# Dealing routing's small VectorE operations out between large ones, with PSUM as a single tile, in a long convolution with routed experts

## Chip, cores and metric

The kernel runs on one core of a Trainium2 chip. The metric is the device time of one execution in microseconds, the median of several.

## What is computed

A long convolution over four batches of 11456 rows by 128 columns, gated by its own input, feeds a mixture of eight experts of which each row takes one. Cut to what matters:

```python
def _attn_ref(x, v, pos_emb, w1, w2):
    h_filt = (np.maximum(pos_emb @ w1, 0.0) @ w2) * np.exp(-0.01 * pos)[:, None]
    u = x * v
    Uf = np.fft.rfft(u, n=2 * S, axis=1)
    Hf = np.fft.rfft(h_filt, n=2 * S, axis=0)
    y = np.fft.irfft(Uf * Hf[None], n=2 * S, axis=1)[:, :S, :]
    return x * y
...
def _moe_ref(x, modality_id, w_gate, modality_bias, w1, w2):
    logits = x @ w_gate + modality_bias[modality_id]
    e_idx = np.argmax(logits, axis=1)
    probs = softmax(logits)
    gate_w = probs[np.arange(N), e_idx]
    for e in range(8):
        mask = e_idx == e
        out[mask] = gate_w[mask, None] * (np.maximum(x[mask] @ w1[e], 0) @ w2[e])
```

## The kernel before

The Fourier transforms are done as matrix products in two levels, an outer one and a middle one. The program is a row of stages: an outer stage, then a middle stage (which works on the spectrum), then the next outer stage, and so on over the four batches, and the experts at the end. An outer stage b does two things at once: the inverse outer transform of batch b - 1, with its gating and its routing, and the forward outer transform of batch b. Three of them (b = 1, 2, 3) are full; the first has only a forward half, the last (b = 4) only an inverse half.

A full outer stage has 16 steps, t = 0 to 15, and a tail of four. In the code, q is such a step's block and o a group, two blocks that are routed together. Each step has on TensorE:
- `turn`: 16 transposes of the middle stage's result into PSUM (wt, L694), which ScalarE copies out (L695);
- `half`: eight transposes of gated rows (xT, L751), copied out by ScalarE (L753);
- `forward`: 64 small matmuls (s, L495), copied out as A (L498);
- `inverse`: py, eight records (L703).

VectorE makes the product of two loaded tiles ready for `forward` (`product`: mul, add, sub, L480, L483, L484), and from py the inverse result: add, sub and the gate with x (L707, L708, L709); the gate writes one of the three buffers xo. Before the add ScalarE copies half of py to y (L706).

Every two steps one group is routed. TensorE computes the logits pl (L759) and turns them (lt, L766), VectorE adds the bias (lg, L772). Then `choice` (L775) runs on VectorE in one piece: mx (L780), dl (L782, written over lg), sco (L787), mb (L789), oh (L790), sc (L792), se (L796), sum (L797) and inv (the reciprocal, L802), with exp (L784) and the row numbers tok (L800) on ScalarE. oh marks the chosen expert of each row, sc its running count. `send` (L813) sums both over the rows on TensorE (pr, L818 to L823); VectorE makes places out of it: ro (L825), base (L826), ro2 (L827) and ix (L829). SP stores the gated rows (`store`, L809, which gives xo back) and the places (`places`, L837), and loads the tiles of coming steps (L475, L688).

The order of the work is set by a table, OUTER, that gives each of these functions a number of steps after its block and a place in the step; a Timeline sorts by them, and each engine runs its instructions in that order. `paced` (L459) ties the scattering of rows of an earlier batch, on GpSimd, to certain VectorE operations.

```python
OUTER = ("turn0:0 turn1:0 lturn:3 biased:3 half:2 product:0 forward:1 choice:3 "
         "inverse:0 logits:2 send:4 load_x:-1 load:-2 store:4 places:5")
...
banks.append(cv.enter_context(tc.tile_pool(name="ps", bufs=4, space=PSUM)))
pairs = cv.enter_context(tc.tile_pool(name="pp", bufs=2, space=PSUM))
```

PSUM is given out by these two pools: four single banks, in turn, to every user of `bank` (wt, xT, pl, lt, pr), and two pairs of banks to the users of `pair` (s, py).

## Time and profile before

| | us |
|---|---|
| median of three runs | 2072.83 |
| lowest and highest | 2069.47, 2073.29 |
| the profiled execution, its own time | 2074.09 |
| its span in the trace | 2072.3 |
| TensorE busy | 1958.3 (94%) |
| VectorE busy | 1752.4 (85%) |
| ScalarE busy | 1284.4 (62%) |
| GpSimd busy | 1169.4 (56%) |
| mean granted TensorE clock | 0.982 |

The profile is of one execution. Its span leaves out the little that lies before the first and after the last recorded instruction. An engine's share is an average over stages that differ; the timelines and the stretches below show single stages.

### The profile page before, as it was taken

The numbers are of one execution on the slowest core, as the hardware profiler recorded it, in microseconds if no ns is written. First come the engines' busy times: TensorE is split into PE (matmuls) and PEld (weight loads), VectorE is DVE, ScalarE is ACT, GpSimd is POOL, SyncE is SP. The second block draws the span as 40 slices with busy tenths as digits, with TensorE's granted clock in tenths as the row PEclk, the third lists the DMA queues.
The fourth block names the chain that finished last, engine by engine and source line by source line (L and its number), as shares of the span: only waits on it lengthen the run. The fifth ranks groups of instructions, "written<-read, shape, count | busy, mean of one in ns | idle before, by whom it ended". The sixth has DMA issues, their size and how long they took to land. (4 is left out here: it accounts for less than half of the span.)

```text
span 2072.3 us, 50243 instructions
## 1 busy us (share of the span) xinstructions
PE 1958.3 (94%) x17646; PEld 1554.1 (75%) x17646; DVE 1752.4 (85%) x2612; ACT 1284.4 (62%) x2404; POOL 1169.4 (56%) x1054
## 2 busy tenths in 40 slices
PE   8899898999989998999789999999999999999997
PEld 8688665776667665776468888877888888888897
DVE  6599899999999899996678888897888778878886
ACT  5555675457744675456456666666666666666675
POOL 0144004766678476974456678786555555555654
PEclk9999999999999999999899999999999999999998
DMA  8565688889988898856787456654645555555421
GB/s 319 184 191 173 231 280 268 268 264 314 327 270 253 280 339 288 283 183 179 199 248 205 97 127 138 133 124 103 118 97 97 97 100 98 96 98 100 86 40 29
DMA packets 610842, 379.46 MB, mean 183 GB/s; under 512 B 424026, under 2 KB 542005, under 8 KB 610585
## 3 DMA queue, kind: packets, MB, share of 16 engines
q1 hardware_dynamic: 587193, 328.61, 58.2%
q0 software_dynamic: 23104, 47.34, 6.6%
q8 instruction: 141, 2.31, 0.5%
q14 instruction: 116, 0.95, 0.2%
q10 hardware_dynamic: 288, 0.25, 0.1%
HBM read 272.74 MB, written 103.70 MB: 182 GB/s over the span
## 5 line engine op out<-in xcount | busy, mean ns | idle before, releaser
L1094 ACT ACTIVATE hh<-ph 128x512 fp32r<-128x512 f32 x724 | 434.0, 599 | 323.2 <-PE ph L1091 320.2
L1095 DVE SCALAR_TENSOR_TENSOR hl<-ph,hh 128x512 fp32r<-128x512 f32 x724 | 488.5, 680 | 164.4 <-ACT hh L1094 155.6
L276 POOL DMA_INDIRECT xs<-back,to x360 | 405.4, 1126 | 319.9 <-DVE se L797 107.9
L1160 POOL DMA_INDIRECT out<-ot,x x362 | 373.3, 1031 | 160.2 <-issue 36.7
L1089 PE MATMUL ph<-xh,wh 128*128 128x512 f32 (+1 forms) x792 | 298.0, 376 | 8.3 <-ACT wh L1060 8.3
L1091 PE MATMUL ph<-xl,wh 128*128 128x512 f32 (+1 forms) x792 | 296.2, 374 | 9.0 <-POOL xl L1077 9.0
L1115 PE MATMUL po<-hl,wh 128*128 128x512 f32 (+1 forms) x792 | 295.6, 373 | 0.9 <-DVE hl L1095 0.6
L1090 PE MATMUL ph<-xh,wl 128*128 128x512 f32 (+1 forms) x792 | 295.6, 373 | 0.0
L1113 PE MATMUL po<-hh,wh 128*128 128x512 f32 (+1 forms) x792 | 295.1, 373 | 0.2 <-ACT hh L1094 0.2
L1114 PE MATMUL po<-hh,wl 128*128 128x512 f32 (+1 forms) x792 | 294.7, 372 | 0.0
L673 ACT COPY A<-pw 128x512 f32<-128x512 f32 (+1 forms) x184 | 97.1, 580 | 188.1 <-PE pw L669 188.1
L1077 POOL TENSOR_TENSOR xl<-xT,xh 128x512 fp32r<-128x512 f32 (+1 forms) x77 | 96.2, 1250 | 203.2 <-ACT xh L1073 203.2
L669 PEld LDWEIGHTS pw<-work 64*128 64x128 f32 x2856 | 167.2, 189 | 32.1 <-ACT work L607 19.2
L625 PE MATMUL pz<-A,work 128*64 128x256 f32 x1440 | 181.1, 394 | 8.3 <-DMA work<-in_c_to 5.0
L638 POOL TENSOR_TENSOR work<-work 128x512 f32<-128x512 f32 (+1 forms) x92 | 115.3, 1253 | 129.0 <-DVE work L634 128.4
L669 PE MATMUL pw<-work 64*128 64x128 f32 x2856 | 181.6, 279 | 4.7 <-POOL work L655 4.3
L1091 PEld LDWEIGHTS ph<-xl,wh 128*128 128x128 f32 x792 | 150.5, 190 | 37.0 <-POOL xl L1077 10.8
L1089 PEld LDWEIGHTS ph<-xh,wh 128*128 128x128 f32 x792 | 150.5, 190 | 33.6 <-ACT wh L1060 8.5
L1115 PEld LDWEIGHTS po<-hl,wh 128*128 128x128 f32 x792 | 150.0, 189 | 29.8 <-DVE hl L1095 4.2
L1090 PEld LDWEIGHTS ph<-xh,wl 128*128 128x128 f32 x792 | 150.6, 190 | 26.1 <-DVE wl L1061 0.4
L1113 PEld LDWEIGHTS po<-hh,wh 128*128 128x128 f32 x792 | 150.0, 189 | 26.1 <-ACT hh L1094 0.7
L1114 PEld LDWEIGHTS po<-hh,wl 128*128 128x128 f32 x792 | 150.0, 189 | 25.7
(181 smaller groups left out, 3613.9 us busy)
## 6 DMA issues: line engine op xcount, KB each, us to landing
work<-hs SPq DMA_DIRECT2D x66, 512.0 KB
work<-in_x SPq DMA_DIRECT2D x64, 512.0 KB
work<-in_xd SPq DMA_DIRECT2D x58, 512.0 KB
work<-in_v SPq DMA_DIRECT2D x51, 512.0 KB
xr<-xo SPq DMA_DIRECT2D x64, 365.6 KB
back<-xr SPq DMA_DIRECT2D x120, 195.0 KB
work<-in_c_to SPq DMA_DIRECT2D x88, 256.0 KB
blocks<-xs SPq DMA_DIRECT2D x328, 64.0 KB
```

The source lines that it names most:

```text
L276: s = pool.indirect_dma_start(out=xs, out_offset=bass.IndirectOffsetOnAxis(ap=ix, axis=0), in_=src, in_offset=None, bounds_check=E * R - 1 ...
L625: pe.matmul(z[64 * s:64 * s + 64, t, r], k["b"][:, t, s, r], A[:, :, 4 * g + 2 * t + s], start=True, stop=True)
L669: pe.matmul(v[s][:, t, blk], k[of][at, t, r, blk], k["c"][at, t, r], start=i == 0, stop=i == len(terms) - 1)
L1089: pe.matmul(p, k[0, "h"][:, f:f + D], k["xh"], start=True, stop=False)
L1090: pe.matmul(p, k[0, "l"][:, f:f + D], k["xh"], start=False, stop=False)
L1091: pe.matmul(p, k[0, "h"][:, f:f + D], k["xl"], start=False, stop=True)
L1094: act.activation(hh, ph, AF.Relu)
L1095: steps.append(ins_of(dve.scalar_tensor_tensor(hl, ph, 0.0, hh.bitcast(F32), op0=ALU.max, op1=ALU.subtract)))
L1113: pe.matmul(po, k[1, "h"][:, f], hh[:, t], start=g == 0, stop=False)
L1114: pe.matmul(po, k[1, "l"][:, f], hh[:, t], start=False, stop=False)
L1115: pe.matmul(po, k[1, "h"][:, f], hl[:, t], start=False, stop=g == NCH - 1)
L1160: s = pool.indirect_dma_start(out=out, out_offset=bass.IndirectOffsetOnAxis(ap=ix, axis=0), in_=src, in_offset=None, bounds_check=N - 1, o ...
```

## The change

The full outer stages no longer use the table for their compute. A function step(t) writes each step's instructions in an order written out by hand; loads, stores and places stay in the table. The first and last outer stages keep the table.

*VectorE.* `product`, the inverse, `choice` and `send` are given as lists of single operations, which step(t) interleaves: between two of the large operations (three of the product, three of the inverse) stands one, at times two, of the small ones. One group's routing now takes two steps. In the even step: mx and dl, with the sums (ro, base, ro2, ix) of the group before; in the odd step: sco, se, mb, sum, oh, inv, sc. Before, all of `choice` stood in the even step, and the sums after the odd step's gate. In the two pieces below, of VectorE in the middle of a full stage, L480 to L484 (after: L505 to L507) are the product, L787 to L802 (after: L840 to L860) the routing, and L746 is the inverse's add. Before:

```order
L480 TENSOR_TENSOR work<-work 128x1024 [waits DMAHW2_49,DMAHW1_49]
L483 TENSOR_TENSOR work<-work 128x512 [waits DVE_49]
L484 TENSOR_TENSOR work<-work 128x512
L780 TENSOR_REDUCE mx<-lg 109x16
L782 TENSOR_TENSOR lg<-lg,mx 109x128 [waits DVE_49]
L787 SCALAR_TENSOR_TENSOR sco<-lg,small 109x128 [waits DVE_49]
L789 TENSOR_REDUCE mb<-sco 109x16 [waits DVE_49]
L790 SCALAR_TENSOR_TENSOR oh_102<-sco,mb 109x128 [waits DVE_49]
L792 SCALAR_TENSOR_TENSOR sc_104<-small,oh_102 109x128 [waits DVE_49]
L796 TENSOR_REDUCE se<-ex 109x16 [waits Activation_49]
L797 TENSOR_SCALAR se<-se 109x16 [waits DVE_49]
L802 RECIPROCAL xo_91<-se 109x4x4 [waits DVE_49]
```

After, from ix of the even step to the odd step's add:

```order
L896 TENSOR_REDUCE ix_94<-ro 109x4x4
L505 TENSOR_TENSOR work<-work 128x1024 [waits DMAHW7_49,DMAHW6_49]
L840 SCALAR_TENSOR_TENSOR sco<-lg,small 109x128 [waits DVE_49]
L855 TENSOR_REDUCE se<-ex 109x16 [waits Activation_49]
L506 TENSOR_TENSOR work<-work 128x512 [waits DVE_49]
L849 TENSOR_REDUCE mb<-sco 109x16 [waits DVE_49]
L856 TENSOR_SCALAR se<-se 109x16 [waits DVE_49]
L507 TENSOR_TENSOR work<-work 128x512
L850 SCALAR_TENSOR_TENSOR oh_102<-sco,mb 109x128 [waits DVE_49]
L860 RECIPROCAL xo_91<-se 109x4x4 [waits DVE_49]
L852 SCALAR_TENSOR_TENSOR sc_104<-small,oh_102 109x128 [waits DVE_49]
L746 TENSOR_TENSOR work<-psum,work 128x512 [waits Activation_49]
```

The seven operations from sco to sc have moved from the even step into the odd step, between the three of the product; inv comes ahead of sc; ix now stands after the even gate.

*TensorE.* pr stays in the odd step, behind py and pl; sc is now computed in the same step. On TensorE at the odd step's end (py is L703, after L735; pl L759, after L808; pr L818 to L823, after L883 to L888; wt L694, after L719) before:

```order
L703 MATMUL py<-work,inv 64x512 x3
L759 MATMUL pl<-work,wg 32x436 x4
L818 LDWEIGHTS both
L818 MATMUL pr<-oh_102,both 128x128
L820 LDWEIGHTS both
L820 MATMUL pr<-sc_104,both 128x128
L823 LDWEIGHTS both
L823 MATMUL pr<-sc_104,both 128x8
L694 MATMUL wt<-ident,A 90x128 x8
L694 MATMUL wt<-ident,A 90x128 [waits Activation_49]
```

After:

```order
L735 MATMUL psum<-work,inv 64x512 x3
L808 MATMUL psum<-work,wg 32x436 [waits Activation_49] x2
L808 MATMUL psum<-work,wg 32x436 x2
L883 LDWEIGHTS both
L883 MATMUL psum<-oh_102,both 128x128 [waits DVE_49]
L885 LDWEIGHTS both
L885 MATMUL psum<-sc_104,both 128x128 [waits DVE_49]
L888 LDWEIGHTS both
L888 MATMUL psum<-sc_104,both 128x8
L719 MATMUL psum<-ident,A 90x128 [waits Activation_49]
```

The order is the same, but pr's matmuls with oh and with sc have become waits for VectorE, and wt waits for ScalarE once for each half.

*PSUM.* One tile holds all eight banks, and each user has banks of its own: pairs in banks 0 to 3, singles in 4 to 7, in the full outer stages wt and s in pairs of 4 to 7, py always in banks 0 and 1, xT in 2 and 3, pl and lt in 2, pr in the last columns of 3.

*Forms.* wt is copied by two copies of 1024 columns a step (before: four of 512). The xT transposes of 109 rows become two, of 64 and of 45 rows, so 16 in a step, in two banks, with one copy for each bank.

The buffers of mx, mb and se go from two to one; ro shares a buffer with sco, before with ex. The diff, cut:

```diff
-        banks.append(cv.enter_context(tc.tile_pool(name="ps", bufs=4, space=PSUM)))
-        pairs = cv.enter_context(tc.tile_pool(name="pp", bufs=2, space=PSUM))
+        psum = cv.enter_context(tc.tile_pool(name="ps", bufs=1, space=PSUM)).tile(
+            [D, 8, 512], F32, name="psum")
...
+        def single(name):
+            return psum[:, 4 + next_of("single", 4)]
+
         def pair(name):
-            return pairs.tile([D, 2, 512], F32, tag="pp", name=name)
+            at = 2 * next_of("pair", 2)
+            return psum[:, at:at + 2]
+
+        def upper(name):
+            at = 4 + 2 * next_of("upper", 2)
+            return psum[:, at:at + 2]
...
-                    p = pair("s1")
+                    p = (upper if b else pair)("s1")
...
             def turn(q, blk):
+                last = b == nb - 1
+                p = None if last else upper("wt")[0:N1]
                 for c in range(2):
-                    p = bank("wt")
+                    pc = bank("wt")[0:N1] if last else p[:, c]
                     for j in range(4):
-                        pe.transpose(p[0:N1, D * j:D * j + D], A[:, blk, :, 8 * q + 2 * j + c], ident)
-                    act.copy(w_t[q % 2][blk][:, c], p[0:N1])
+                        pe.transpose(pc[:, D * j:D * j + D], A[:, blk, :, 8 * q + 2 * j + c], ident)
+                    if last:
+                        act.copy(w_t[q % 2][blk][:, c], pc)
+                if not last:
+                    act.copy(w_t[q % 2][blk], p)
...
-                py = pair("py")
+                py = psum[:, 0:2]
...
             def turn(o, half):
...
+                rows = (slice(0, 64), slice(64, PU))
+                pt = [psum[:, 2 + k, 0:8 * (at.stop - at.start)].rearrange("p (w h n) -> p w h n", w=2, h=4)
+                      for k, at in enumerate(rows)]
                 for way in range(2):
-                    pt = bank("xT")
                     for h in range(4):
-                        pe.transpose(pt[:, PU * h:PU * h + PU], xo[0:PU, way, half, h, 0:D],
-                                     ident[0:PU, 0:PU])
-                    act.copy(xT_t[:, 2 * way + half].rearrange("p h n -> p (h n)"),
-                             pt[:, 0:4 * PU])
+                        for p, at in zip(pt, rows):
+                            pe.transpose(p[:, way, h], xo[at, way, half, h, 0:D], ident[at, at])
+                xT = xT_t.rearrange("p (w s) h n -> p w s h n", w=2)[:, :, half]
+                for p, at in zip(pt, rows):
+                    act.copy(xT[:, :, :, at], p)
...
-            line.stages(at, NQ, LAST if b == nb else OUTER, todo,
-                        lambda name: 2 if name in LATE else 0, when)
+            if b == nb:
+                line.stages(at, NQ, LAST, todo, lambda name: 2 if name in LATE else 0, when)
+                return
+            line.stages(at, NQ, OUTER, {n: todo[n] for n in LATE}, lambda name: 2, when)
+            line.put(at - 2, lambda: product(0))
+            line.put(at - 1, lambda: product(1))
+            chosen, sums = {}, {}
+
+            def step(t):
+                o, odd = t // 2 - 2, t % 2
+                here = 0 <= o < NO
+                if t < NQ:
+                    turn(t, 0)
+                    turn(t, 1)
+                if 0 <= t - 2 < NQ:
+                    rturn((t - 2) // 2, t % 2)
+                if here and odd:
+                    chosen["exp"]()
+                    chosen["tok"]()
+                if 0 <= t - 1 < NQ:
+                    transform(t - 1)
+                if here and not odd:
+                    lturn(o)
+                p = psteps(t) if 2 <= t < NQ else [lambda: None] * 3
+                c = lambda *names: [chosen[n]() for n in names] if here and odd else None
+                r = lambda k: sums.pop(k)() if k in sums and not odd else None
+                p[0](), c("sco", "se"), r(0)
+                p[1](), c("mb", "sum"), r(1)
+                p[2](), c("oh", "inv", "sc"), r(2)
+                if here and not odd:
+                    biased(o)
+                    chosen.update(csteps(o))
+                i = isteps(t) if t < NQ else [lambda: None] * 3
+                e = lambda name: chosen[name]() if here and not odd else None
+                i[0](), e("mx")
+                i[1](), e("dl")
+                i[2](), r(3)
+                if odd and 0 <= (t - 3) // 2 < NO and t >= 3:
+                    logits((t - 3) // 2)
+                if here and odd:
+                    sums.update(enumerate(ssteps(o)))
+                    if t > NQ:
+                        for k in range(4):
+                            sums.pop(k)()
+
+            for t in range(TAIL + 1):
+                line.put(at + t, lambda t=t: step(t))
```

## Rows read from the trace of the kernel before

**Rows 1.** The page's first part: busy time, share of the span, instructions by engine
```profile
PE 1958.3 (94%) x17646; PEld 1554.1 (75%) x17646; DVE 1752.4 (85%) x2612; ACT 1284.4 (62%) x2404; POOL 1169.4 (56%) x1054
```

**Rows 2.** The stretches view: length, busy (count) by engine, TensorE clock, DMA share, GB/s
```profile
sum 313.79, PE 300.25 PEld 205.41 DVE 283.30 ACT 231.51 POOL 138.19; mean PE 100.08 PEld 68.47 DVE 94.43 ACT 77.17 POOL 46.06
...
298.77:313.07 14.30, 13.84 (x219) 9.56 (x210) 13.79 (x26) 10.85 (x22) 0.00 (x0) 1.00 0.78 271
500.51:558.85 58.34, 55.66 (x840) 38.34 (x832) 55.09 (x104) 43.66 (x86) 40.89 (x32) 1.00 0.96 327
732.56:790.73 58.17, 55.44 (x840) 38.33 (x832) 55.12 (x104) 43.65 (x85) 42.21 (x32) 1.00 0.98 338
229.59:270.13 40.54, 39.13 (x603) 27.45 (x603) 34.28 (x58) 30.73 (x60) 0.00 (x0) 1.00 0.73 249
```

**Rows 3.** VectorE's timeline in one pair: start, duration, line, tiles, count [idle before]
```profile
302.45 0.69 DVE L707 TENSOR_TENSOR work<-py,work 128x512 f32<-128x512 f32 x1
...
305.76 0.38 DVE L829 TENSOR_REDUCE ix<-ro 109x16 int32<-109x128 f32 x1
...
306.25 1.22 DVE L480 TENSOR_TENSOR work<-work 128x1024 f32<-128x1024 f32 x1
...
308.11 0.69 DVE L484 TENSOR_TENSOR work<-work 128x512 f32<-128x512 f32 x1
308.71 0.36 DVE L780 TENSOR_REDUCE mx<-lg 109x16 f32<-109x128 f32 x1
309.11 0.29 DVE L782 TENSOR_TENSOR lg<-lg,mx 109x128 f32<-109x128 f32 x1
...
311.68 0.63 DVE L707 TENSOR_TENSOR work<-py,work 128x512 f32<-128x512 f32 x1
...
313.07 1.23 DVE L709 TENSOR_TENSOR xo<-work 128x1024 f32<-128x1024 f32 x1
```

**Rows 4.** TensorE's timeline of the same pair (a row may hold several instructions)
```profile
299.85 1.94 PE L703 MATMUL py<-work,inv 90*64 90x512 f32 x8 [0.20 <-ACT A L498]
...
302.65 0.22 PE L820 MATMUL pr<-sc,both 109*128 109x128 bf16 x1
...
302.74 2.11 PE L694 MATMUL wt<-ident,A 128*90 128x128 f32 x16
304.68 0.66 PE L766 MATMUL lt<-ident,work 128*109 128x128 f32 x4
305.18 1.03 PE L751 MATMUL xT<-ident,xo 109*128 109x109 f32 x8
306.14 1.47 PE L495 MATMUL s<-fwd,work 64*64 64x90 f32 x64
307.87 1.94 PE L703 MATMUL py<-work,inv 90*64 90x512 f32 x8 [0.26 <-ACT A L498]
```

**Rows 5.** Timelines of VectorE and TensorE in the first stage's tail
```profile
347.60 0.42 DVE L792 TENSOR_TENSOR_SCAN sc<-small,oh 109x128 bf16<-109x128 f32 x1
...
347.63 0.29 PE L818 MATMUL pr<-oh,both 109*128 109x128 bf16 x1 [4.99 <-DVE oh L790]
348.08 0.27 PE L820 MATMUL pr<-sc,both 109*128 109x128 bf16 x1 [0.17 <-DVE sc L792]
```

**Rows 6.** SP's and VectorE's timelines in stages two and three: stores and gates
```profile
534.23 1.80 SPq L809 DMA_DIRECT2D xr<-xo  x2
...
544.65 1.23 DVE L709 TENSOR_TENSOR xo<-work 128x1024 f32<-128x1024 f32 x1 [0.67 <-DMA xr<-xo]
...
766.76 1.83 SPq L809 DMA_DIRECT2D xr<-xo  x2
...
776.02 1.23 DVE L709 TENSOR_TENSOR xo<-work 128x1024 f32<-128x1024 f32 x1
```

**Rows 7.** TensorE's timeline in a middle stage
```profile
400.58 2.95 PE L669 MATMUL pw<-work 64*128 64x128 f32 x48
```

**Rows 8.** ScalarE's timeline in the pair of rows 3
```profile
303.50 2.06 ACT L695 COPY work<-wt 90x512 f32<-90x512 f32 x4 [0.17 <-PE wt L694]
```

More of the change, by code (lines that the diff above doesn't have):

```diff
@@ L200, in bank @@
     def bank(name):
+        if callable(banks[-1]):
+            return banks[-1](name)
         return banks[-1].tile([D, 512], F32, tag="ps", name=name)
@@ L499, in transform @@
                              p[:, :, 0:4 * N1].rearrange("p b (n k) -> p b k n", n=4))
-            return load, product, transform
+            return load, product, transform, product_steps
         def filter_stages():
@@ L763, in logits_turn @@
             def logits_turn(o):
-                pt = kept[o] = bank("lt")
+                pt = kept[o] = psum[:, 2]
                 for h in range(4):
@@ L775, in choice, with choice_steps @@
             def choice(o):
+                steps = choice_steps(o)
+                for name in ("mx", "dl", "exp", "sco", "mb", "oh", "sc", "se", "tok", "sum", "inv"):
+                    steps[name]()
+            def choice_steps(o):
                 i = b * NO + o
@@ L792, in choice, with first_of_best @@
-                dve.tensor_tensor_scan(
-                    sc[0:PU].rearrange("p e c -> p (e c)"), sm("keep")[0:PU],
-                    oh[0:PU].rearrange("p e c -> p (e c)"), 0.0, op0=ALU.mult, op1=ALU.add)
-                se = rt.tile([PU, NC], F32, tag="se", name="se")
-                dve.tensor_reduce(se, ec(ex), axis=AX.X, op=ALU.add)
-                dve.tensor_scalar_add(se, se, 1e-9)
+                own = {}
+                def first_of_best():
+                    own["sco"] = rt.tile([PU, E, NC], F32, tag="sco", name="sco", bufs=1)
+                    dve.scalar_tensor_tensor(own["sco"], lg, 0.0, fst, op0=ALU.is_ge, op1=ALU.mult)
@@ L798, in choice @@
                 xov = xo[0:PU].rearrange("p w s h r -> p h (w s) r")
                 by_h = lambda t: t.rearrange("p (h g) -> p h g", h=4)
-                act.activation(xov[:, :, :, D + 1].bitcast(I32), by_h(sm("tok")[0:PU]), AF.Copy,
-                               bias=float(b * S + 8 * o))
-                paced(dve.reciprocal(xov[:, :, :, D], by_h(se)))
+                return {
+                    "mx": lambda: dve.tensor_reduce(mx, ec(lg), axis=AX.X, op=ALU.max),
+                    "dl": lambda: dve.tensor_sub(lg, lg, wide(mx)),
+                    "exp": lambda: act.activation(ex, lg, AF.Exp),
+                    "sco": first_of_best,
+                    "mb": lambda: dve.tensor_reduce(mb, ec(own["sco"]), axis=AX.X, op=ALU.max),
+                    "oh": lambda: dve.scalar_tensor_tensor(
+                        oh[0:PU], own["sco"], 0.5, wide(mb), op0=ALU.max, op1=ALU.is_equal),
+                    "sc": lambda: dve.tensor_tensor_scan(
+                        sc[0:PU].rearrange("p e c -> p (e c)"), sm("keep")[0:PU],
+                        oh[0:PU].rearrange("p e c -> p (e c)"), 0.0, op0=ALU.mult, op1=ALU.add),
+                    "se": lambda: dve.tensor_reduce(se, ec(ex), axis=AX.X, op=ALU.add),
+                    "sum": lambda: dve.tensor_scalar_add(se, se, 1e-9),
+                    "tok": lambda: act.activation(
+                        xov[:, :, :, D + 1].bitcast(I32), by_h(sm("tok")[0:PU]), AF.Copy,
+                        bias=float(b * S + 8 * o)),
+                    "inv": lambda: paced(dve.reciprocal(xov[:, :, :, D], by_h(se)))}
@@ L813, in send, with send_steps @@
             def send(o):
+                for f in send_steps(o):
+                    f()
+            def send_steps(o):
                 i = b * NO + o
                 oh, sc = oh_t[i % 2], sc_t[i % 2]
-                pr = bank("pr")
+                if banks[-1] is single:
+                    pr = psum[:, 3, 512 - E * NC - E:512]
+                else:
+                    pr = bank("pr")
                 prv = pr[:, 0:E * NC].rearrange("p (e c) -> p e c", e=E)
@@ L839, in places @@
                         ix[64 * blk:64 * blk + HALF].rearrange("p (w m) -> p w m", w=2))
-            return turn, logits, logits_turn, biased, choice, send, store, places
+            return turn, logits, logits_turn, biased, choice, send, store, places, choice_steps, send_steps
         def every_other(f):
@@ L862, in outer @@
             if b < nb:
-                load, product, transform = forward_stages(b)
+                load, product, transform, psteps = forward_stages(b)
                 todo |= {"load": load, "product": product, "forward": transform}
@@ L894, in hyena_moe_kernel @@
         todo = filter_stages()
-        load, todo["product"], todo["forward"] = forward_stages(0)
+        load, todo["product"], todo["forward"], _ = forward_stages(0)
         for name in ("xd", "v"):
```

84 lines of the change are left out of this document (50 added, 34 removed).

## The prediction

> **What bounds the kernel now.** The page's first part comes first: TensorE is busy 94% of the span, VectorE 85% [rows 1]. These are averages over stages with different limits, so next I cut out the stages that the change touches, the three full outer stages, with the view of busy time by stretch: from first to last gate they take 313.79 us together [rows 2], so nothing outside them and their tails can move. After about six steps each settles to a fixed period of two steps (a pair, which routes one group): 14.30 us in the first stage, 58.34 / 4 = 14.59 and 58.17 / 4 = 14.54 in the other two [rows 2]. In the 14.30 us TensorE is busy 13.84 and VectorE 13.79: both nearly full, each waiting now and then for the other. DMA share is 0.78 in the first stage, 0.96 to 0.98 in the others, and TensorE's clock is granted in full in these windows, so the clock is no part of this.
>
> VectorE's timeline shows how a pair is filled [rows 3]. Where an operation does not need its predecessor, it starts about 0.09 us before that one ends (308.11 + 0.69 = 308.80, but mx starts at 308.71). Where it reads the predecessor's result, it starts 0.03 to 0.04 us after the end (308.71 + 0.36 = 309.07, dl at 309.11). So a dependent neighbour costs about 0.12 us more than an independent one.
>
> **VectorE's part of the change.** The two orders show 15 dependent neighbours in a pair before (two in each product and inverse, the rest inside the routing), and 2 after (add to sub to gate of the odd step's inverse). 13 x 0.115 = 1.5 us a pair: VectorE's chain falls from some 14.2 to 12.7 us. If VectorE alone were the bound, 24 pairs would give 36 us. It is not alone.
>
> **TensorE's part.** The xT transposes go from 8 with 109 moving columns, 306.14 - 305.18 = 0.96 us [rows 4], to 16 with 64 and 45, which I call X for one step. No row shows this form, so it is bounded. The nearest row has the same stationary shape (64 x 128) in two row groups, with 128 moving columns: 48 in 2.95 us, some 60 ns each [rows 7]. If moving columns set that time, eight pairs of halves cost 8 x 60 = 0.48 us; if loading the weights does, 16 x 60 = 0.96. The s row bears on it: 64 matmuls with 64 stationary columns take 307.87 - 306.14 - 0.26 = 1.47 us [rows 4], 23 ns each, so twice the columns need at most 46 ns or 0.74 us. I take 0.6, half-way between 0.48 and 0.74, and keep 0.48 and 0.96 as ends. The Trainium skill, "TensorE: Matmul & The Clock Gate", section LDWEIGHTS, says that a weight load costs its columns over 1.2 in nanoseconds and that fewer rows save nothing; with 16 loads of 128 columns in two row groups that would be, as an estimate, 16 x 107 / 2 = 0.85 us. The 60 ns of [rows 7] agree with that page as well as with moving columns, so the row decides nothing between them. TensorE's own work in a pair becomes 13.84 - 2 x 0.93 + 2 x 0.6 = 13.2 us, which is also less than 14.3.
>
> **The new wait.** What decides is where sc now ends. Before, the second half of the routing ran in the even step, and its prefix sums on TensorE (pr) came in the odd step, when sc was long done. Now sco to sc are dealt over the odd step, and pr stands behind py and pl of the same odd step, ahead of the next step's wt. TensorE takes its instructions in order: in the stage's tail it stood 4.99 us in front of pr for oh, and started its second matmul 0.06 us after sc ended (347.60 + 0.42 = 348.02, then 348.08) [rows 5]. Behind pr wait wt, xT, s, lt and py, and behind py waits VectorE's next inverse. That closes a loop of one pair:
> - From the even step's first inverse operation to the end of sc, VectorE runs 16 operations: one inverse, mx, dl, ix, one product, sco, se, mb, sum, oh, inv, sc. The old order has the same ones without ix in a row, 15 of them from 306.25 to the gate that starts at 313.07 and gives way 1.14 later: 7.96 us, 10 of the hand-overs dependent [rows 3]. Without those, 7.96 - 10 x 0.115 = 6.81; ix adds 0.38 - 0.09 = 0.29; and sc counts to its end, 0.09 more: 7.2.
> - Hop to pr 0.06, pr's rest 302.74 - 302.65 = 0.09, wt 1.9 (304.68 - 302.74 = 1.94 here, 1.85 in the other step), X, s 1.47, lt 305.18 - 304.68 = 0.50 [rows 4].
> - py's start to the inverse on VectorE: 302.45 - 299.85 = 2.60 [rows 3, 4].
>
> The sum is 13.82 + X: **14.42 us with X = 0.6**, 14.30 to 14.78 between the ends. So VectorE's saving does not shorten the pair; it turns into a VectorE wait for y of 14.4 - 12.7 = 1.7 us a pair, and TensorE waits for sc.
>
> **PSUM and the merged copies.** The second half of s now writes the banks that the second wt copy empties. Four copies of 512 columns take 2.06 us [rows 8]; as two, I keep 2.06, starting when half of wt (0.93) is done, so done some 3.1 us after wt begins, while s' second half begins at 1.9 + X + 0.74: an X below 0.5 gains nothing. py on one pair of banks waits for the add and sub of the step before, which end some 1.3 us after sc, while wt, xT, s and lt hold py back for 4.6: nothing, and in the odd step the cover is still over a microsecond. ro waits for the xT copies on its bank, by the same 1 ns a column 0.15 + 3.1 + 0.9 = 4.1 us after sc, where VectorE arrives after the odd inverse and p0, 2.6 + 1.1 = 3.7: a few tenths, which come out of its wait for y. exp and tok lie on ScalarE, 10.85 of 14.30 busy [rows 2], before se needs them.
>
> **The store.** inv now comes 5.15 us after the even gate's start (the 7.2 without add and sub, 313.07 - 311.68 - 2 x 0.115 = 1.16, mx 0.27, dl 0.20 and sc 0.42 [rows 3, 5]). The store of a group follows inv on SP's queue, and with three buffers the next even gate needs that one back. Before, inv came a step earlier. In the second stage a store issued at 534.23 gave its buffer back at 544.65, 10.42 later, and VectorE waited 0.67 for it; in the third stage the gate at 776.02 came 9.26 after the issue without a wait [rows 6]. So the second loop is 5.15 + 9.3 to 10.4 = 14.4 to 15.6 in stages 2 and 3. I take 14.7 there, nearer the lower end because only a single gate of [rows 6]'s stage waited at all; the emptier first stage is left to the first loop. places now also waits for ix behind the even gate; behind it on SP stand the loads of the odd step, which have a ring of four units of slack: nothing, or part of the high end.
>
> **The sum.** First six steps: 40.54 us, of which TensorE idles 1.4 [rows 2]; those waits and the smaller xT, which enters from the third step on, give 1.4 to 2.7 back; I take 1.6. But the odd gate of a pair now has seven small operations, sco to inv, in front of it: from dl's end at 309.40 to the add at 311.68 they took 2.28, less six dependent hand-overs 1.6 [rows 3], and that gate comes as much later: zero together. Steady pairs, four a stage: 4 x 0.12 = 0.5 in the first, 4 x (14.7 - 14.56) = 0.5 in each other. Tails: the last group's routing stands a little later before the next stage's products; I choose 0.3 each, between 0 and 0.7. 0.5 + 0.5 + 0.5 + 0.9 = +2.4 us on the profiled execution's 2074.09, which lies 1.26 above the median of 2072.83: **2075 us**, no change that can be told; 0.2% is 4.1 us.
>
> **Rivals.**
> - *The dealing pays in full*: pr does not hold TensorE, and the pair falls to its own 13.2 us. 4 x 1.1 + 8 x 1.35 = 15, with the early steps up to 20: 2053 to 2058. Against it stand the order of pr ahead of wt and [rows 5]. Chance 0.08.
> - *The loop comes out short*: wt 1.85, X 0.5, VectorE's run 7.1, the hop to y 2.55 give 14.1, stages 2 and 3 lose their waits for TensorE's irregular turns (14.56 to 14.2), and the early 1.6 are kept in part. 4 x 0.2 + 8 x 0.4 + 3 = 7: 2064 to 2068. Chance 0.16.
> - *The store loop binds* in stages 2 and 3: slower. Its price is 10.42 + 5.15 - 14.56 = 1.0 a pair, 8 us over eight pairs, plus tails: 2080 to 2084. It decides from a store latency of 9.3 us. For it: DMA share 0.96 and up, and a gate that waited already; against: most stores of before were back without a wait. Chance 0.22.
> - *Weights set xT's time*, X = 0.85 to 0.96: the pair is 14.67 to 14.78, 0.4 to 0.5 over stage 1 and 0.1 to 0.2 over the others, 4 x 0.4 + 8 x 0.2 + 0.9 = 4: 2077 to 2079. The page cited above would have it so. Chance 0.2, over half of it past 0.2%.
> - The forecast itself: 0.34.
>
> **Numbers.** Faster: 0.08 + 0.16 = 0.24. Slower: 0.22 + 0.12 = 0.34. The rest, 0.42, is within 0.2%. The range leaves out the full gain and the worst store latency: 2064 to 2085.
>
> **What would show it.** Right: pairs of 14.3 to 14.7 between gates; a wait of pr's second matmul for sc in each pair; VectorE waiting 1 to 2 us a pair for y, its small operations without idle around them; in stages 2 and 3 gates that wait for the store. The second rival shows as the same waits with shorter pairs. Wrong: pairs near 13.2 without a wait at pr; xT far from 0.5 to 0.9 us a step; a merged copy over 1.1 us; or time moved outside the three stages.

## The result: slower by 1.1%

The changed kernel takes 2093.79 us, the median of four runs (2088.04 to 2100.29), the kernel before 2071.15 (2067.58 to 2073.29) beside it: a ratio of 1.0112, 95% interval 1.0075 to 1.0149, or 22.6 us more. The profiled execution of the change took 2090.47 us, with a span of 2088.7 us and a mean granted TensorE clock of 0.976 (before: 0.982).

The stretches view says where the time went. First the change: the three full outer stages, from first to last gate, each followed by the stretch to the next outer stage's first gate, which holds the stage's tail and the middle stage. (Columns as in [rows 2].)

```profile
230.27:332.28 102.01, 97.03 (x1618) 65.52 (x1614) 87.93 (x167) 74.85 (x121) 5.13 (x4) 1.00 0.78 265
332.28:459.31 127.03, 114.29 (x1489) 87.68 (x1484) 117.36 (x117) 59.19 (x109) 92.77 (x82) 0.97 0.84 270
459.31:569.51 110.20, 101.80 (x1632) 69.25 (x1626) 88.56 (x167) 75.91 (x121) 58.91 (x54) 0.95 0.89 301
569.51:700.35 130.84, 117.26 (x1490) 89.20 (x1486) 117.39 (x118) 59.26 (x109) 91.47 (x79) 0.93 0.80 258
700.35:812.08 111.73, 100.24 (x1630) 68.10 (x1626) 88.43 (x167) 75.47 (x121) 58.25 (x54) 0.97 0.88 295
812.08:945.41 133.33, 117.58 (x1442) 89.22 (x1434) 122.60 (x119) 58.61 (x112) 104.51 (x86) 0.95 0.76 243
```

The same three stretches between the stages, before:

```profile
332.55:459.96 127.41, 116.42 (x1483) 89.60 (x1481) 118.44 (x118) 60.24 (x113) 89.91 (x79) 0.97 0.83 265
565.17:690.42 125.25, 114.73 (x1455) 87.98 (x1446) 118.83 (x119) 59.56 (x112) 91.13 (x78) 0.97 0.84 270
796.04:924.74 128.70, 118.01 (x1453) 88.99 (x1451) 124.76 (x119) 59.00 (x112) 106.80 (x85) 0.97 0.79 249
```

| | before | after | difference |
|---|---|---|---|
| stage 1, first to last gate | 102.96 | 102.01 | -0.95 |
| to the next first gate | 127.41 | 127.03 | -0.38 |
| stage 2 | 105.21 | 110.20 | +4.99 |
| to the next first gate | 125.25 | 130.84 | +5.59 |
| stage 3 | 105.62 | 111.73 | +6.11 |
| to the next first gate | 128.70 | 133.33 | +4.63 |

The six differences add up to 20.0 us. Two things are to be seen. Stage 1's steady pairs came out as they were worked out, and those of stages 2 and 3, with the same instructions, did not. And half of the loss lies after the last gate, where the change moved only a group's routing and the PSUM banks; there TensorE's granted clock is 0.93 and 0.95, before 0.97. (The rest of the program, from the last gate of all, took 1053.48 us instead of 1057.46; the kernel before took 1055.4 there in another profiled execution, so much of this is spread.)

**Stage 1: the loop through pr.** TensorE and then VectorE in one pair of the change:

```profile
301.69 0.22 PE L883 MATMUL psum<-oh,both 109*128 109x128 bf16 x1 [0.61 <-DVE oh L850]
302.14 0.22 PE L885 MATMUL psum<-sc,both 109*128 109x128 bf16 x1 [0.24 <-DVE sc L852]
...
302.23 1.98 PE L719 MATMUL psum<-ident,A 128*90 128x128 f32 x16
304.14 0.71 PE L800 MATMUL psum<-ident,xo 64*128 64x64 f32 x16
304.77 1.47 PE L518 MATMUL psum<-fwd,work 64*64 64x90 f32 x64
...
306.79 1.94 PE L735 MATMUL psum<-work,inv 90*64 90x512 f32 x8
```

```profile
295.05 0.69 DVE L746 TENSOR_TENSOR work<-psum,work 128x512 f32<-128x512 f32 x1 [1.10 <-ACT work L738]
...
301.71 0.38 DVE L852 TENSOR_TENSOR_SCAN sc<-small,oh 109x128 bf16<-109x128 f32 x1
...
306.32 0.29 DVE L892 TENSOR_TENSOR ro<-psum,base 109x128 f32<-109x128 f32 x1 [0.53 <-ACT work L803]
...
309.43 0.69 DVE L746 TENSOR_TENSOR work<-psum,work 128x512 f32<-128x512 f32 x1 [1.14 <-ACT work L738]
```

The pairs, from even gate to even gate, are 14.40 us, three times running, and then 14.45. TensorE waits 0.61 us for oh and 0.24 for sc, then runs wt (302.23 to 304.14, 1.91), xT (304.14 to 304.77, X = 0.63), s, lt and py; VectorE waits 0.53 us for the xT copy ahead of ro and 1.14 for y. From the add at 295.05 to sc's end at 302.09 are 7.04 us (7.2 in the prediction), from py at 306.79 to the next add at 309.43 2.64 (2.60). The small operations now stand without idle between the large ones: VectorE is busy 87.93 us in the stage where it was 94.50 us, and the stage is only 0.95 us shorter.

**Stages 2 and 3: the gate waits for the store.** Pairs there are 15.63, 17.00, 16.76, 15.99 and 18.09, 15.97, 16.97, 15.98 us. VectorE's gates and SP's queue in stage 2:

```profile
513.02 1.23 DVE L742 TENSOR_TENSOR xo<-work 128x1024 f32<-128x1024 f32 x1 [1.09 <-DMA xr<-xo]
...
530.02 1.23 DVE L742 TENSOR_TENSOR xo<-work 128x1024 f32<-128x1024 f32 x1 [0.95 <-DMA xr<-xo]
```

```profile
502.81 1.76 SPq L867 DMA_DIRECT2D xr<-xo  x2
...
514.55 2.46 SPq L905 DMA_DIRECT2D xi<-ix  x2
...
518.66 0.38 SPq L493 DMA_DIRECT2D work<-in_v  x1
519.14 1.76 SPq L867 DMA_DIRECT2D xr<-xo  x2
```

What SP's queue waited for between 500 and 560 us (us in total, times, longest):

```profile
SPq L905 <- DVE ix L896: 14.2, 3, 5.9
```

The store issued at 502.81 gives its buffer back at 513.02, 10.21 us later [rows 6]; the next, issued at 519.14, at 530.02, 10.88 later. From the gate at 513.02 to that store's issue are 6.12 us; 6.12 + 10.88 is the pair of 17.00. In between stand on SP the places at 514.55: they wait up to 5.9 us for ix, which now stands behind the waiting gate (in the kernel before, SP waits for ix nowhere between 500 and 560 us), and only behind them come the step's loads (the last at 518.66) and the store. inv was through at 518.05. In the five pairs of the two stages that end with a gate that had to wait, the way from gate to store took 5.42 to 6.47 us and the store 10.2 to 11.6.

**What the wait sets off.** The late gate makes sc late, so TensorE waits longer in front of pr, and after that its clock is lower:

```profile
534.95 0.22 PE L883 MATMUL psum<-oh,both 109*128 109x128 bf16 x1 [1.66 <-DVE oh L850]
...
535.56 2.90 PE L719 MATMUL psum<-ident,A 128*90 128x128 f32 x16
538.39 1.11 PE L800 MATMUL psum<-ident,xo 64*128 64x64 f32 x16
```

```profile
534.50:541.00 6.50, 5.74 (x99) 4.98 (x98) 4.85 (x10) 3.42 (x5) 4.31 (x5) 0.74 0.90 261
```

After 1.66 us of waiting for oh, and 0.31 for sc, wt takes 538.39 - 535.56 = 2.83 us, where in stage 1 it took 1.91; the mean granted clock of the stretch is 0.74. The late y that follows is added to pairs whose gate does not wait: in stage 3, after a wait of 4.24 us at pr, the next pair took 15.97 us with no wait at its even gate.

**The tails.** TensorE and VectorE behind the last gate of stage 2 in the change, and TensorE there in the kernel before:

```profile
582.33 3.68 PE L648 MATMUL psum<-A,work 128*64 128x256 f32 x16 [4.42 <-DVE lg L821]
591.95 0.27 PE L883 MATMUL psum<-oh,both 109*128 109x128 bf16 x1 [5.93 <-DVE oh L850]
...
592.61 3.68 PE L648 MATMUL psum<-A,work 128*64 128x256 f32 x16
596.22 2.84 PE L692 MATMUL psum<-work 64*128 64x128 f32 x32
```

```profile
589.57 0.69 DVE L675 TENSOR_TENSOR work<-work 128x512 f32<-128x512 f32 x1
...
591.61 0.28 DVE L850 SCALAR_TENSOR_TENSOR oh<-sco,mb 109x128 bf16<-109x128 f32 x1
```

```profile
580.24 0.29 PE L818 MATMUL pr<-oh,both 109*128 109x128 bf16 x1 [4.99 <-DVE oh L790]
...
580.90 3.68 PE L625 MATMUL pz<-A,work 128*64 128x256 f32 x16
584.51 2.91 PE L669 MATMUL pw<-work 64*128 64x128 f32 x32
```

From the last gate, at 569.51 (the end of the change's third stretch), to the first pw: 596.22 - 569.51 = 26.7 us, before 584.51 - 565.17 = 19.3 (the start of the second of the three stretches before). pz waits 4.42 us for VectorE's lg, because the middle stage's pair of banks now comes to lie on lt's bank, and pr waits 5.93 us for oh, whose operations now stand behind the middle stage's second products on VectorE (the last of these at 589.57). Both pz rows take 3.68 us for 16 records, where 16 at full clock take 1.95: half speed, the lower of the clock's two levels (1.2 GHz).

### The profile page after: what moved, and what is told of

Same layout as the page of the kernel before. It is cut to its first block, busy times and chain, and to the rows that moved or that the text cites. A ratio compares the mean times of both kernels' runs of the same rounds, so it can differ in the third digit from the quotient of the medians.

```text
span 2088.7 us, 50650 instructions
## 1 busy us (share of the span) xinstructions
PE 1952.9 (93%) x18030; PEld 1547.7 (74%) x18030; DVE 1724.4 (83%) x2612; ACT 1274.9 (61%) x2308; POOL 1152.7 (55%) x1054
## 5 line engine op out<-in xcount | busy, mean ns | idle before, releaser
L278 POOL DMA_INDIRECT xs<-back,to x360 | 388.5, 1079 | 338.2 <-DVE lg L846 109.7
L696 ACT COPY A<-psum 128x512 f32<-128x512 f32 (+1 forms) x184 | 97.1, 579 | 206.4 <-PE psum L692 206.4
L648 PE MATMUL psum<-A,work 128*64 128x256 f32 x1440 | 183.2, 398 | 7.6 <-DVE lg L821 4.4
L692 PEld LDWEIGHTS psum<-work 64*128 64x128 f32 x2856 | 166.7, 189 | 29.1 <-ACT work L630 19.6
L692 PE MATMUL psum<-work 64*128 64x128 f32 x2856 | 180.3, 279 | 2.6 <-POOL work L678 2.3
```

Of the source, the lines that this page charges most:

```text
L278: s = pool.indirect_dma_start(out=xs, out_offset=bass.IndirectOffsetOnAxis(ap=ix, axis=0), in_=src, in_offset=None, bounds_check=E * R - 1 ...
L648: pe.matmul(z[64 * s:64 * s + 64, t, r], k["b"][:, t, s, r], A[:, :, 4 * g + 2 * t + s], start=True, stop=True)
L692: pe.matmul(v[s][:, t, blk], k[of][at, t, r, blk], k["c"][at, t, r], start=i == 0, stop=i == len(terms) - 1)
```

## The experiments

Theory A: in stages 2 and 3 the xo buffer sets the pair, through inv and through SP's queue. B: TensorE's clock at pr does it alone. C: the scatter's transfers do. D: the tail costs its own part, by the banks (D1) or by the order on VectorE (D2). All pairs and gaps (last gate to next first gate) below are read from gates in the profile.

**Places one step later.**

```diff
-         "inverse:0 logits:2 send:4 load_x:-1 load:-2 store:4 places:5")
+         "inverse:0 logits:2 send:4 load_x:-1 load:-2 store:4 places:6")
```

> Edit: in the full outer stages the stores of places (which wait for ix) are issued one step later, behind the step's loads and the store of xo on SP's queue. Theory A (the xo buffers): in stages 2 and 3 the pair is as long as the way from a gate to the next store plus the 10 to 11.6 us until that store gives its buffer back, and SP's queue is part of that way: places stand there behind ix and hold the loads and the store up, 6.1 us from gate to store where inv alone would take 5.0. Then pairs in stages 2 and 3 fall from 16.0 to 18.1 to about 15.5, the two stages by 5 to 8 us together, stage 1 stays at 14.40 a pair. Theory B (TensorE's clock falls while it waits at pr for sc, and the slow wt and xT make the long pairs, whatever the store does): pairs stay at 16 and over. Theory C (the scatter's DMA load alone): no change.

2098.75 us, ratio 1.0134 (1.0117 to 1.0151). Pairs of 14.47, 15.17, 16.08, 14.55 and 15.36, 14.46, 14.77, 14.55: stages 2 and 3 fall to 108.04 and 106.38 us, 7.5 together, as expected of A and against B and C, although their last gates now waited 2.98 and 2.77 us for a load of x. But the gaps grew to 133.7, 132.9 and 137.2 with a clock of 0.90 to 0.91, so the whole was slower than the change.

**inv early.**

```diff
-                p[0](), c("sco", "se"), r(0)
-                p[1](), c("mb", "sum"), r(1)
-                p[2](), c("oh", "inv", "sc"), r(2)
+                p[0](), c("se", "sum", "inv", "sco"), r(0)
+                p[1](), c("mb"), r(1)
+                p[2](), c("oh", "sc"), r(2)
```

> Edit: se, sum and inv stand directly behind the odd step's product mul instead of spread over it, so that inv ends some 1.9 us earlier. Theory A with SP's queue as the longer way (6.1 us against 5.0): nothing to gain, stages 2 and 3 within 2 us of the change. If inv is the longer way: pairs of about 14.5 in stages 2 and 3, some 12 us together. Theories B and C: no change. Stage 1: pairs 0.2 longer at most (three dependent neighbours more).

2103.12 us, 1.0145 (1.0126 to 1.0164). Stages 2 and 3 stay at 109.96 and 111.07: inv was not the longer way, SP's queue was. Here too the gaps grew, to 133.6, 133.4 and 135.3.

**Both.**

> Edit: both, places one step later and inv early. Theory A: gate to store falls to about 3.6 us, plus 10.3 makes 13.9, so the first loop (14.4 to 14.6) sets the pair in all three stages; stages 2 and 3 fall by 10 to 12 us together, TensorE's granted clock stays at 1.00 in them, and the wait at pr goes back to the 0.6 to 0.9 us of stage 1. Theory B: pairs of 16 and clock below 1.00 remain. Theory C: no change.

2102.69 us, 1.0136 (1.0116 to 1.0155). Pairs of 14.73 to 14.83 in all three stages, clock 1.00 in all of them, no gate that waits for xo: A is shown inside the stages, B falls. (The 0.35 over 14.40 fit the three dependent neighbours of se, sum and inv, at some 0.12 us each.) The two stages fall by 9.0 us, less than the 10 to 12 expected: their last gates waited 2.89 and 1.30 us for x. The gaps, 135.6, 134.8 and 137.3, again ate it up.

**The tail as before the change.** The last group's routing runs whole ahead of the second products; its lt and pr get single banks.

```diff
-                pt = kept[o] = psum[:, 2]
+                pt = kept[o] = bank("lt") if not last and o == NO - 1 else psum[:, 2]
...
+                if t == TAIL - 1:
+                    for n in ("mx", "dl", "exp", "sco", "mb", "oh", "sc", "se", "tok", "sum", "inv"):
+                        chosen[n]()
                 i = isteps(t) if t < NQ else [lambda: None] * 3
```

> Edit: in the stage's tail only: the last group's routing runs whole in one step, ahead of the second products, as before the change, and its lt and pr get single banks away from the middle stage's pairs. Theory D (the tail): the way from the last gate to the first pw goes from 23.8, 26.7 and 26.4 us back to about 19 to 20, and the stretches from last gate to the next stage's first gate fall by 3 to 6 us in stages 2 and 3 (now 130.8 and 133.3, before 125.3 and 128.7); stage 1's is absorbed already. Rival (the stretches are longer for what stage 2 and 3 leave behind, clock and scatter): no change of more than 2 us.

2079.07 us, 1.0038 (1.0023 to 1.0052). Gaps of 125.0, 124.2 and 128.8 with clock 0.97, pairs of 16 as in the change. The tail is worth about two thirds of the loss. TensorE behind stage 2's last gate here, with pz on time and pr's wait back at the 4.99 us of before:

```profile
574.25 1.95 PE L648 MATMUL psum<-A,work 128*64 128x256 f32 x16
581.19 0.26 PE L883 MATMUL psum<-oh,both 109*128 109x128 bf16 x1 [4.99 <-DVE oh L850]
```

**Of the tail, the banks alone** (the first of these changes, and pr's bank with it).

> Edit: of the tail's two parts only the banks: lt and pr of the stage's last group get single banks away from the middle stage's pairs; the second half of its routing stays behind the second products. Theory D1 (the tail's cost is the wait of pz for the banks, 4.42 us in stage 2's tail, and of lt, 3.6 in the others): gaps from last gate to next first gate back to 125 to 129 us as in the run with both parts (125.0, 124.2, 128.8). Theory D2 (it is pr's wait for oh, which now stands behind the second products on VectorE, 6 us during which TensorE does nothing, and the lower clock after it): gaps stay at 130 to 137 with a mean granted clock of 0.90 to 0.95.

2093.16 us, 1.0099 (1.0082 to 1.0116); gaps of 128.0, 130.7 and 133.1. D1 alone falls: with the order left, the banks give nothing back. What TensorE no longer waits ahead of lt and pz it waits at pr, 9.62 us in the tails of stages 1 and 2, where in the change's stage 1 it was 3.58 at lt and 5.97 at pr. In stage 1:

```profile
353.17 0.27 PE L883 MATMUL psum<-oh,both 109*128 109x128 bf16 x1 [9.62 <-DVE oh L850]
```

**pr one step later.** pr is issued in the next even step, behind wt.

```diff
+                if not odd and 0 <= o - 1 < NO and t <= NQ:
+                    sums.update(enumerate(ssteps(o - 1)))
                 if 0 <= t - 2 < NQ:
                     rturn((t - 2) // 2, t % 2)
...
-                if here and odd:
+                if here and odd and t > NQ:
                     sums.update(enumerate(ssteps(o)))
```

> Edit: pr moves from the odd step's end to the next even step, behind wt, so that TensorE's wt no longer waits for sc; all else as changed. Theory A (first loop through pr; store loop in stages 2 and 3): stage 1's pair falls from 14.40 to between TensorE's own 13.2 and 13.6 us; in stages 2 and 3 the store loop remains, pairs of 15.5 to 17. Theory B (clock lost at pr makes stages 2 and 3 long): pairs fall to 14 in all three. Gaps as in the change or longer.

2091.36 us, 1.0088 (1.0071 to 1.0105). Stage 1's steady pairs go to 13.5 to 14.3, now with waits for the store there too, and not to the 13.2 to 13.6 expected; stages 2 and 3 keep pairs of 15.7 to 17.5, apart from one of 14.0. The gaps are 130.2, 130.8 and 135.4. So both loops are there, and whichever is longer shows.

**All of these together, and all but pr.**

> Edit: the tail's two parts, places one step later, inv early, and pr one step later. By theories A and D together: pairs of 13.2 to 13.6 in stage 1, 13.6 to 14.2 in stages 2 and 3 (store loop 3.6 + 10.3), gaps of 124 to 129, so 2052 to 2062 us, faster than the kernel before by 0.5 to 1%. If pr's wait is not what holds the pair: 14.4 to 14.8 everywhere and about 2068.

> Edit: the tail's two parts, places one step later and inv early; pr where the change put it. By theories A and D: pairs of 14.75 in all stages, gaps of 124 to 129, so some 2068 to 2072 us, the time of the kernel before: the dealing gains nothing as long as pr stands in the odd step. If the gaps lengthen as they did with the store's edits alone (133 to 137): 2090 and over.

2078.22 us, 1.0025 (1.0014 to 1.0037), and 2084.03 us, 1.0054 (1.0035 to 1.0073): 16 and 12 us over the upper ends of what was expected. With pr later the steady pairs are 13.0 to 14.8, without it 14.75 mostly (the longest 16.3), about as expected; the gaps are 129.5 to 132.4 in spite of the tail. SP's queue at the end of stage 1 in the first of the two shows why:

```profile
315.62 4.04 SPq L905 DMA_DIRECT2D xi<-ix  x2
322.35 0.34 SPq L265 DMA_DIRECT2D to<-xi  x1
...
325.83 2.34 SPq L711 DMA_DIRECT2D work<-in_x  x1
```

The fetch of the places (to<-xi) comes directly behind the places written one step late, and SP stands from 319.66 to 322.35 until they have landed; behind it waits the last x, for which the last gate then waited 3.19 us. This was my edit's own fault. Where the last gate is late, the long gaps follow: in stage 1 of the first three runs it waited 1.5, 0.7 and 0.8 us for x, and the gaps there were 133.7, 133.6 and 135.6, with the clock at 0.91 to 0.92; in the change it did not wait, and the gap was 127.0 at 0.97. In the second of those three, inv early, whose places were in their step, TensorE's clock fell already at the tail's first waits (1.15, 0.72 and 0.43 us one after another), and all that followed in the tail ran slower. It is not a rule: the run with the banks alone had a last gate 1.3 us late and a gap of 128.0. Why x was late in the run with inv early stays open, and so does why the gap is long after one late gate and not after another. Between the two runs of this paragraph, which differ only in pr's place, pr one step later is worth 5.8 us.

**ix early instead of places late.** ix goes ahead of the even gate, so the places stay in their step; se, sum and inv are dealt ahead of the product's add with no dependent neighbours.

```diff
-                i[0](), e("mx")
+                i[0](), r(3), e("mx")
                 i[1](), e("dl")
-                i[2](), r(3)
+                i[2]()
...
+                p[0](), c("se", "sco", "sum", "mb", "inv"), r(0)
+                p[1](), c("oh"), r(1)
+                p[2](), c("sc"), r(2)
```

Four kernels with it, or beside it, ran in one go:

> Edit: tail as before the change (whole routing ahead of the second products, banks of its own), ix ahead of the even gate (so places on SP no longer stand behind it and stay in their step), se, sum and inv ahead of the product's add, dealt so that no neighbour is dependent, and pr one step later. By theories A and D, with the late load of the last x gone (the runs with places a step later stopped SP at the fetch of places written just before): pairs of 13.3 in stage 1, 13.3 to 14 in stages 2 and 3, gaps of 124 to 129 with granted clock 0.96 to 0.97, so 2050 to 2060 us, some 0.7% faster than the kernel before. If the gaps come back at 130 to 132 with clock 0.93: 2068 to 2075.

> Edit: only ix ahead of the even gate, and se, sum and inv ahead of the product's add, all else as changed: the store's way cleared without delaying places. Theory A: pairs of 14.3 to 14.5 in all stages with clock 1.00, so stages 2 and 3 fall from 110.2 and 111.7 to 102 to 104; gaps as in the change (127, 131, 133): some 2078 to 2082 us. If instead the earlier runs' clean stages came from places being late: pairs of 16 stay.

> Edit: as the run before, and the tail as before the change; pr in the odd step. Theories A and D: pairs of 14.3 to 14.5, gaps of 124 to 129: 2062 to 2070 us, 0.1 to 0.5% faster than the kernel before. Against the run with pr later, it gives what pr's place is worth: 24 pairs of about 1 us, of which 12 to 18 us.

> Edit: the change without the dealing: VectorE's order, the sums' place and lt's place as before, with the single PSUM tile, the split xT and the merged wt copies kept (lt in bank 0). Theory A (PSUM and the forms cost nothing, dealing with pr's wait and the store is the cause): pairs of 14.2 to 14.3 in stage 1, 14.2 to 14.6 in the others, gaps near 125 to 129, so 2066 to 2074 us. Theory E (the shared banks cost time in the steady pairs too): pairs over 14.6, or gaps over 130.

They came to a chip on which the kernel before took 2119.44 us (2107.39 to 2130.72). Ratios: 1.0009 (0.9988 to 1.003), 1.0081 (1.0055 to 1.0108), 0.9993 (0.9971 to 1.0015), 1.0013 (0.9991 to 1.0035). In stage 1 the pairs were as expected (13.3, 14.4, 14.4, 14.2), in stages 2 and 3 they were 15.6 to 19.4 in the three dealt kernels and 16.0 to 16.1 in the undealt one, at this DMA share and rate (last two columns):

```profile
500.30:548.50 48.20, 44.01 (x672) 29.48 (x671) 41.59 (x79) 31.80 (x51) 27.88 (x25) 1.00 0.94 309
```

In the kernel before, the first chip moved 327 to 338 GB/s at a share of 0.96 to 0.98 [rows 2]. I took it that transfers set the pair on this chip, and that TensorE stops inside s for loads; the traces don't show that. In three pairs of the undealt kernel VectorE, which reads what is loaded, waits for no load, and TensorE's seven stops inside s (1.9 us) are for nothing that the profile shows. The same kernel on a later chip, in stage 3, had three pairs of 14.2 us at a DMA share of 1.00 and 348 GB/s, more than here. What makes this chip slower stays open. What this set shows is the tail once more: the second and third kernel differ only in it, by 18.7 us. The first and third differ only in pr's place, and their times are the same (2120.27 and 2119.29 us).

So three of the four ran again, beside the kernel before as a control:

> The kernel before, unchanged, profiled beside the next three. On the chip of the last four runs its time was 2119 us instead of 2072, and pairs of 16.0 us in stages 2 and 3 appeared even with VectorE's old order, with TensorE waiting inside s for loads. If transfers set the pair there: this profile shows pairs near 16 wherever its time is near 2119, and near 14.55 wherever it is near 2072, with the DMA share at 0.95 or more in both.

> Edit: as in the run with the tail as before, ix ahead of the even gate, inv early and pr one step later. Theories A and D: where the kernel before takes about 2072, pairs of 13.3 in stage 1 and 13.3 to 14.3 in stages 2 and 3, gaps of 124 to 130, and 0.5 to 0.8% faster. Where transfers set the pair (before at 2119): no difference in stages 2 and 3, within 0.3% of the kernel before.

> Edit: only ix ahead of the even gate and inv early, tail and pr as changed. Theory A where the kernel before takes about 2072: pairs of 14.3 to 14.5 in all three stages, no waits for xo at the gates; gaps of 127 to 137 with a clock of 0.90 to 0.95 remain (theory D), so 2080 to 2092 us. Otherwise pairs near those of the kernel before on the same chip.

> Edit: the change without the dealing (VectorE's order as before; PSUM tile, split xT and merged wt copies kept). Theory A: pairs of 14.2 in stage 1 and within 0.3 us of the kernel before on the same chip in the others, and a time within 0.3% of it. Theory E (the shared banks cost time by themselves): slower by over 0.5%.

- The kernel before again: 2070.34 us, 0.9992 (0.9978 to 1.0007), pairs of 14.2 to 15.0. What it does on the slower chip was not seen.
- ix and inv early only: 2078.47 us, 1.0037 (1.0021 to 1.0052), 15 us less than the change and a little under what was expected. Pairs of 14.37 to 14.59 in all three stages; the change's 110.20 and 111.73 are now 102.78 and 102.21, with the clock at 1.00, while the gap between them is as long as in the change:

```profile
460.73:563.51 102.78, 97.27 (x1634) 65.70 (x1629) 88.21 (x168) 75.25 (x121) 59.01 (x54) 1.00 0.95 324
563.51:695.36 131.85, 117.34 (x1492) 89.25 (x1487) 118.03 (x119) 59.19 (x109) 91.65 (x79) 0.94 0.81 256
695.36:797.57 102.21, 97.17 (x1629) 65.59 (x1622) 87.94 (x167) 75.17 (x121) 58.48 (x54) 1.00 0.97 329
```

VectorE and SP in stage 2 show the cleared way: ix at 512.03, places at 512.59 ahead of the gate at 513.43, the store at 517.53, 4.1 us after the gate:

```profile
512.03 0.40 DVE L896 TENSOR_REDUCE ix<-ro 109x16 int32<-109x128 f32 x1
...
513.43 1.21 DVE L742 TENSOR_TENSOR xo<-work 128x1024 f32<-128x1024 f32 x1
```

```profile
512.59 1.76 SPq L905 DMA_DIRECT2D xi<-ix  x2
...
517.53 2.42 SPq L867 DMA_DIRECT2D xr<-xo  x2
```

- The change without the dealing: 2081.57 us, 1.0047 (1.0031 to 1.0064). Pairs of 14.17 to 14.24 in stages 1 and 3, and one of 17.89 in stage 2; gaps of 131.0, 129.4 and 131.8. The time lies between the 0.3% of theory A and the 0.5% of theory E, and E holds for the tail alone: with the old order but shared banks, lt and pr wait for the products there (TensorE behind stage 2):

```profile
580.08 1.16 PE L815 MATMUL psum<-ident,work 128*109 128x128 f32 x4 [3.67 <-DVE work L666]
...
588.43 0.22 PE L883 MATMUL psum<-oh,both 109*128 109x128 bf16 x1 [3.58 <-DVE work L666]
```

So the banks and the order are each enough to spoil the tail, which is why mending one gave nothing. In stage 1 the undealt kernel takes 100.29 us:

```profile
230.28:330.57 100.29, 95.53 (x1578) 64.58 (x1570) 93.96 (x168) 75.43 (x120) 5.14 (x6) 1.00 0.79 272
```

The kernel before took 103.23 us there on this chip, and the dealt kernel of the item before this one 102.16; in stage 3 the three take 100.40, 105.39 and 102.21. So the single PSUM tile and the new forms of wt and xT shorten these stages by themselves, and the dealing, with pr in the odd step, makes them longer again.
- All together (tail, ix and inv early, pr later): **2056.50 us, 0.9924 (0.9902 to 0.9946)**, 0.8% faster than the kernel before. Pairs of 13.3 in stage 1 and 12.7 to 15.7 in the others, gaps of 124.8, 124.8 and 129.2:

```profile
232.00:329.85 97.85, 96.79 (x1650) 65.81 (x1646) 87.55 (x168) 75.82 (x122) 6.34 (x5) 1.00 0.83 279
554.29:679.13 124.84, 115.83 (x1473) 88.01 (x1466) 117.69 (x119) 59.13 (x108) 91.33 (x79) 0.96 0.86 272
```

```profile
300.66 2.01 PE L719 MATMUL psum<-ident,A 128*90 128x128 f32 x16
302.51 0.22 PE L883 MATMUL psum<-oh,both 109*128 109x128 bf16 x1
```

In stage 1 TensorE hardly stops: wt runs at 300.66 ahead of pr, and TensorE is busy 96.79 of 97.85 us. How much of the 0.8% the dealing brings is not shown: the three stages take 97.85, 99.68 and 101.58 us here, the undealt kernel's 100.29, 105.60 (with the pair of 17.89) and 100.40, and the undealt kernel with its tail mended was not run. Nor was the dealt one with the tail mended and pr in the odd step run on this chip.

## Why the prediction was wrong

- **The loop through pr**: right. Predicted 13.82 + X = 14.42 with X = 0.6; measured 14.40 with X = 0.63, between the ends of 0.48 and 0.96. VectorE's wait was to be 1.7 us a pair and was 1.14 + 0.53. In stage 1's steady pairs the dealing gains nothing as long as pr holds wt: 14.40 us, where the undealt kernel has 14.2 and the best one, with pr a step later, 13.3. By the rule on weight loads that the Trainium skill gives ("TensorE: Matmul & The Clock Gate", section LDWEIGHTS), a load takes its time by its columns, whatever its rows; the prediction's estimate from it was 0.85 us. The measured 0.63 is less, some 39 ns for each half, so here halves in two row groups did save time.
- **The first six steps**: better than taken. Stage 1 became 0.95 us shorter instead of 0.5 longer: the steps up to the seventh gate took 37.69 us instead of 40.54, 2.85 less where 1.6 was taken. (The odd gate's 1.6 came as forecast: at the stage's end it stands 6.67 us behind the even gate instead of 5.19.) Most of this is not the dealing: the undealt kernel takes 38.4 us for these steps of stage 1.
- **"I take 14.7 there"**, the store loop of stages 2 and 3: this step failed. The way from gate to store was taken at 5.15 us, through inv, and was 5.4 to 6.5, the longer ones through SP; and the buffer came back after 10.2 to 11.6 us, not 9.3 to 10.4. The third rival had the mechanism and, at 15.6 us a pair, too small a price: 15.6 to 18.1 was measured, 15.9 us over the eight pairs where it had 8 (the two stages are 11.1 us longer, as their first six steps are shorter). The sentence "places now also waits for ix ... nothing, or part of the high end" named the right queue and dismissed it: the loads behind the places had slack, but the store behind the loads had none. And the wait's consequence was not priced at all: after its waits of 1.4 to 4.2 us at pr TensorE ran at a lower clock.
- **"Tails ... I choose 0.3 each"**: the largest failure. Measured +5.6 and +4.6 after stages 2 and 3 here, and some 15 us of the whole by the run that mends it. The view of the order had the second half of the last group's routing behind the second products, with pr and pz behind it on TensorE, and the trace of before had a wait of 4.99 us there [rows 5], in stage 2 with 16 pz at half speed behind it (the 3.68 us above); and here a longer wait at such a place cost more than its length.
- **PSUM**: right in the steady pairs (14.2 undealt), wrong in the tail, where pz meets the routing's banks, which the prediction did not price.

## What to carry over

When an instruction moves behind one that can wait, follow each queue that it feeds to the buffer that closes a loop: here ix fed places, places stood ahead of loads, and behind them was the store on which the next gate depended. Dealing out one engine's small operations can't shorten a pair as long as the engine in between waits for the last of them in the same turn: with that consumer issued one step later, stage 1's pairs went from 14.4 to 13.3 us. How much of the final gain that is, and how much the forms alone would give, was not separated. Look at a stage's tail as a stage of its own: with only a few dependent instructions left, a reordering that costs nothing in the steady part can idle TensorE, and the lower clock behind the wait then makes it dearer, as in this tail.

## What was not expected of the hardware

TensorE's granted clock fell to 0.50 in the tail after waits of 4.4 us on top of shorter ones, and 16 pz then took 3.68 instead of 1.95 us; in stage 1 waits of 0.61 + 0.24 us at pr in every pair left it at 1.00, while waits of 1.4 to 4.2 us in stages 2 and 3 brought the stretch behind them to 0.73 to 0.79. And chips differ: the kernel before took 2071 to 2072 us on three of them and 2119 on a fourth, where pairs of the undealt kernel took 16.0 us that take 14.2 elsewhere, so a gain inside a stage can vanish on another chip. What sets the pair there is not shown.
